# Moving the w_out sums from GpSimd to VectorE, and spacing the loads of q, k and v, in a fused attention and SiLU kernel

## The chip, the cores and the metric

The kernel runs on one core of a Trainium2 chip. The time is that of the device in microseconds (us), from several runs each; the kernel before has a median of 400.0 us in its first three runs. A profile is one execution; its span is about 1.7 us shorter than the time of the same run (381.9 against 383.64 us for the changed kernel). TensorE is PE, its weight loads PEld, VectorE DVE, ScalarE ACT, GpSimd POOL, SyncE SP.

## The reference

```python
# q, k, v: 8 batches x 12 heads x 448 positions x 64, float32
scores = (1 / sqrt(64)) * q @ k.T - log(448)
attn   = sigmoid(scores) @ v
x      = attn with heads side by side          # 3584 x 768
h      = x @ w_in                              # 768 x 2048
g      = h * sigmoid(h)
out    = g @ w_out                             # 2048 x 768, out 3584 x 768
```

## The kernel before

Groups of four heads (24 groups, numbered from 0) go through scores, sigmoid and the product with v. A batch of three groups then goes through x @ w_in, the gate, and g @ w_out. The last product is made by a scheme with seven products of quarters instead of eight. It needs sums of quarters of g, for each pair of row blocks (14 times four sums of 128x1024 on VectorE), and sums of quarters of w_out, once. The latter are eight, four for each half of the columns' chunks, and stand on GpSimd:

```python
def tt(key, dur, deps, o, a, b_, op, prio=0):
    pl.op("DVE", dur, key, deps, lambda: nc.vector.tensor_tensor(o, a, b_, op), prio=prio)

def tt_pool(key, n, deps, o, a, b_, op, prio=0):
    pl.op("POOL", 100 + 2.2 * n, key, deps, lambda: nc.gpsimd.tensor_tensor(o, a, b_, op), prio=prio)

def sums_wo(f0, f1):
    ...
    a11, a12, a21, a22 = wo[:, r, :HE], wo[:, r, HE:], wo[:, r2, :HE], wo[:, r2, HE:]
    for z, (o, x_, y_) in enumerate(((t1, a12, a11), (t2, a22, t1), (a12, a22, a12), (t4, a21, t2))):
        dz = dep if z == 0 else [kk + (z - 1,)]
        if z in (0,1,2,3):
            tt_pool(kk + (z,), (f1 - f0) * HE, dz, o, x_, y_, sub, 5)
        else:
            tt(kk + (z,), d, dz, o, x_, y_, sub, 5)
```

All loads of q, k, v and the weights are issued by GpSimd:

```python
def load(key, deps, fn, nd, size):
    first = [("issue", pl.loads)] if pl.loads else []
    pl.loads += 1
    pl.op("POOL", 650, key, deps + first, fn, nbytes=0.872 * nd / 16 * (21 + 0.0368 * size))
```

`pl` is a planner. It keeps a clock in Python, with an assumed duration for every operation, and calls each `fn` when its clock says that the operation's inputs (`deps`) are there and its engine is free. That decides only the order in which instructions enter each engine's queue. The semaphore waits of the program come from the data that instructions share (and from the reuse of semaphores), not from `deps`. This matters for the second part of the change.

## Time and profile before

| | before |
|---|---|
| time, median of the first 3 runs | 400.0 us (399.7 to 401.24) |
| PE busy, share of the span | 375.7 us, 94% |
| DVE busy | 211.1 us, 53% |
| ACT busy | 232.8 us, 58% |
| POOL busy | 90.1 us, 23% |
| mean granted clock of PE | 0.972 |

Shares of the whole span hide the point: VectorE at 53% is no bound. The prediction below therefore starts from the row of forty slices, finds the few where PE is not full, and asks what the other engines did there. One thing to know when reading busy times: an instruction that has started and is held up counts as busy all the while (the sum of 9.30 us below is one; its twins take 0.68). A "busy" VectorE can be a blocked one.

### The profile page before, as it was taken

What the parts mean: (1) busy time and instruction counts of PE and PEld (TensorE: products, weight loads), DVE (VectorE), ACT (ScalarE), POOL (GpSimd) and SP (SyncE); (2) the same over time, 40 slices, a digit from 0 to 9 for tenths busy, and PEclk for the clock granted to TensorE, in tenths of its full rate; (3) what the DMA queues carried; (4) which work ended last, traced back from release to release, by engine and by line L of the source; (5) the groups of instructions that cost most, each with busy time, mean ns of one, the idle gap of its engine ahead of it and who ended that gap; (6) DMA issues with size and microseconds to landing.
All of it is one profiled execution on the core that took longest, in us unless ns stands there. A gap on an engine that the chain in (4) does not pass through costs nothing.

```text
span 400.2 us, 17994 instructions
## 1 busy us (share of the span) xinstructions
PE 375.7 (94%) x8024; PEld 315.7 (79%) x8024; DVE 211.1 (53%) x368; ACT 232.8 (58%) x506; POOL 90.1 (23%) x105
## 2 busy tenths in 40 slices
PE   7999869995999999969999999999999999999995
PEld 3676757893887889958898889887989888988773
DVE  4536694797326447415365254554554545554633
ACT  2994629625787686445955697658647766134110
POOL 9656461892222202202022012220200000000000
PEclk9999968997999999998999999999999999999998
DMA  8999990990599996866688999988875101310235
GB/s 111 200 209 203 211 167 2 139 146 2 72 143 196 214 169 104 118 148 121 71 137 107 185 148 130 140 127 116 131 125 115 24 2 43 82 44 2 52 73 120
DMA packets 80636, 46.51 MB, mean 116 GB/s; under 512 B 50608, under 2 KB 79792, under 8 KB 80560
## 3 DMA queue, kind: packets, MB, share of 16 engines
q0 software_dynamic: 25008, 22.81, 38.4%
q1 hardware_dynamic: 55552, 22.56, 33.7%
q8 instruction: 63, 1.03, 1.0%
q14 instruction: 13, 0.11, 0.1%
HBM read 45.61 MB, written 11.01 MB: 141 GB/s over the span
## 4 chain that ended last, share of the span: by engine, by line
PE 82%; DMA 6%; DVE 5%; ACT 3%; issue 2%; POOL 0%; ACTq 0%; DVEq 0%; POOLq 0%
PE ps L803 31%; PE ps L677 29%; PE ps L502 8%; PE ps L514 8%; PE ps L713 5%; DMA xk<-in_k_dram 5%; DVE gs L276 2%; ACT at L952 2%; DVE gt L624 1%; DMA xq<-in_q_dram 1%; PE ps L985 1%; ACT sg L619 1%; PE ps L460 1%; DVE kT L474 1%; ACT at L545 0%
## 5 line engine op out<-in xcount | busy, mean ns | idle before, releaser
L677 PE MATMUL ps<-xt,wi 64*64 64x448 f16 x2304 | 166.9, 352 | 4.1 <-issue 3.7
L545 ACT ACTIVATE at<-ps 128x448 f16<-128x448 f32 x252 | 122.3, 553 | 50.8 <-PE ps L502 43.3
L677 PEld LDWEIGHTS <-wi 64*64 64x64 f16 x2304 | 114.7, 108 | 17.4 <-issue 6.1
L624 DVE TENSOR_TENSOR gt<-ps,sg 128x448 f16<-128x448 f32 (+2 forms) x128 | 78.0, 621 | 76.6 <-ACT sg L619 76.5
L803 PE MATMUL ps<-wo,gt 64*64 64x384 f16 x1344 | 114.9, 326 | 3.3 <-DVE gt L624 3.3
L803 PEld LDWEIGHTS <-gt 64*64 64x64 f16 x1792 | 98.9, 108 | 15.6 <-issue 5.9
L619 ACT ACTIVATE sg<-ps 128x448 f16<-128x448 f32 (+2 forms) x128 | 69.8, 552 | 63.9 <-PE ps L677 32.6
L803 PEld LDWEIGHTS <-gs 64*64 64x64 f16 x1344 | 78.9, 108 | 8.8 <-issue 0.7
L803 PE MATMUL ps<-so,gs 64*64 64x384 f16 x896 | 83.0, 326 | 0.0
L502 PE MATMUL ps<-qT,kT 64*64 64x448 f16 (+2 forms) x840 | 80.4, 334 | 2.2 <-DVE gt L624 1.1
L817 DVE SCALAR_TENSOR_TENSOR us<-ps,us 128x384 f32<-128x384 f32 x70 | 38.8, 555 | 56.7 <-PE ps L803 46.7
L239 POOL DMA_DIRECT2D v<-in_v_dram x24 | 17.4, 724 | 194.2 <-PE ps L514 77.8
L502 PEld LDWEIGHTS <-kT 64*64 64x64 f16 x840 | 37.5, 112 | 12.7 <-issue 8.1
L952 ACT ACTIVATE at<-ps 128x512 f16<-128x512 f32 (+3 forms) x96 | 39.6, 543 | 10.8 <-PE ps L502 10.7
L803 PE MATMUL ps<-so,gt 64*64 64x384 f16 x448 | 44.6, 323 | 0.1
L514 PE MATMUL ps<-at,v 64*64 64x448 f16 (+2 forms) x840 | 42.1, 322 | 2.7 <-DMA xk<-in_k_dram 1.5
L713 PE MATMUL ps<-xt,wi 128*128 128x256 f16 (+1 forms) x384 | 42.8, 268 | 1.4 <-issue 1.1
L803 PE MATMUL ps<-wo,gs 64*64 64x384 f16 x448 | 43.7, 323 | 0.0
L713 PEld LDWEIGHTS <-wi 128*128 128x128 f16 x384 | 34.8, 101 | 6.6 <-issue 2.8
L514 PEld LDWEIGHTS <-v 64*64 64x64 f16 x840 | 30.9, 110 | 7.3 <-issue 3.6
L824 ACT ACTIVATE us<-ps 128x384 f32<-128x384 f32 x28 | 14.0, 501 | 30.3 <-PE ps L803 30.3
L557 DVE TENSOR_SCALAR xt<-ps 128x448 f16<-128x448 f32 x36 | 20.9, 619 | 17.8 <-PE ps L514 16.2
(33 smaller groups left out, 183.8 us busy)
## 6 DMA issues: line engine op xcount, KB each, us to landing
out_dram<-us SPq DMA_DIRECT2D x112, 96.0 KB, 3.1
xk<-in_k_dram POOLq DMA_DIRECT2D x24, 224.0 KB, 6.2
v<-in_v_dram POOLq DMA_DIRECT2D x24, 224.0 KB, 5.2
xq<-in_q_dram POOLq DMA_DIRECT2D x21, 224.0 KB, 7.3
wo<-in_moe_w_out_dram POOLq DMA_DIRECT2D x4, 768.0 KB, 15.3
wi<-in_moe_w_in_dram POOLq DMA_DIRECT2D x8, 192.0 KB, 7.1
wi<-in_moe_w_in_dram POOLq DMA_DIRECT2D x4, 384.0 KB, 9.5
qT<-xq SPq DMA_TRANSPOSE x32, 4.7
```

The lines of the kernel that those rows point to most:

```text
L239: lambda: nc.gpsimd.dma_start(v16[n % NV], src(v, b, g)),
L502: nc.tensor.matmul(pt[r][64 * h : 64 * h + 64, lo : lo + (c1 - c0) * D], kT[n % NTR][64 * r : 64 * r + 64, i, 64 * h : 64 * h + 64], qT[n ...
L514: nc.tensor.matmul(pt[h][64 * j : 64 * j + 64, :N], v16[n % NV][64 * h : 64 * h + 64, j, c * D : (c + 1) * D], at[64 * h : 64 * h + 64, sl ...
L545: lambda r=r: nc.scalar.activation(at[:, sl, r], pt[r][:, :S], AF.Sigmoid, bias=NEG_LOG_S, scale=QKSCALE),
L557: lambda h=h: nc.vector.tensor_scalar_mul(x[:, 2 * g + h, :], pt[h][:, :S], SX), prio=-2,
L619: lambda: nc.scalar.activation(t[:, :ncol], src_, AF.Sigmoid, scale=ISX), prio=0,
L624: lambda: nc.vector.tensor_tensor(o, src_.rearrange("p (a t) -> p a t", a=nb), t[:, :ncol].rearrange("p (a t) -> p a t", a=nb), ALU.mult),
L677: nc.tensor.matmul(bank[64 * j : 64 * j + 64, z * N : z * N + N], wi[64 * h : 64 * h + 64, cc, f0 + 64 * j : f0 + 64 * j + 64], x[64 * h : ...
L713: nc.tensor.matmul(bank[:, z * N : z * N + N], wi[:, cc, fc * P : (fc + 1) * P], x[:, cc, self.c0 : self.c1], start=(cc == 0 and z == 0), ...
L803: nc.tensor.matmul(bank[64 * j : 64 * j + 64, :HE], lhs[64 * h : 64 * h + 64, c, 64 * j : 64 * j + 64], rhs[64 * h : 64 * h + 64, c, :], s ...
L817: lambda: nc.vector.scalar_tensor_tensor(o, bank[:, :HE], ISX, u, ALU.mult, ALU.add), prio=-2,
L952: lambda r=r, src_=src_: nc.scalar.activation(at[:, base : base + m, r, :N], src_, AF.Sigmoid, bias=NEG_LOG_S, scale=QKSCALE),
```

## The change

The intent: take the eight sums off GpSimd, and let each load from the tenth group (number 9) on be issued only when the load before has landed, so that transfers come one after another.

```diff
+    last_load = [None]
+
     def load(key, deps, fn, nd, size):
 
         first = [("issue", pl.loads)] if pl.loads else []
+        if key[0] in ("k", "q", "v") and key[1] >= 9:
+            first.append(last_load[0])
+        last_load[0] = key
         pl.loads += 1
         pl.op("POOL", 650, key, deps + first, fn, nbytes=0.872 * nd / 16 * (21 + 0.0368 * size))
@@
-            if z in (0,1,2,3):
+            if z in ():
                 tt_pool(kk + (z,), (f1 - f0) * HE, dz, o, x_, y_, sub, 5)
             else:
                 tt(kk + (z,), d, dz, o, x_, y_, sub, 5)
```

## The prediction

> **What bounds the kernel now.** I read the page's row of slices first: it says where, not only how much. Each digit is a tenth of a 10 us slice.
>
> ```profile
> PE   7999869995999999969999999999999999999995
> DVE  4536694797326447415365254554554545554633
> POOL 9656461892222202202022012220200000000000
> PEclk9999968997999999998999999999999999999998
> ```
>
> TensorE (PE) is at 9 nearly everywhere, so it is the bound. It falls to 6 in the sixth slice (50 to 60 us), to 5 in the tenth (90 to 100) and to 6 in the eighteenth, and the granted clock dips with or just after each. In the first two VectorE (DVE) and GpSimd (POOL) are both near full. The table by stretch puts numbers on it; columns are start:end, length, busy PE, PE loads, DVE, ACT, POOL with counts, clock, DMA share, GB/s.
>
> ```profile
> 45.00:57.00 12.00, 8.30 (x136) 6.79 (x136) 10.99 (x11) 5.45 (x12) 9.67 (x3) 0.85 1.17 209
> 57.00:65.00 8.00, 7.06 (x103) 5.58 (x106) 4.56 (x10) 4.87 (x11) 0.00 (x0) 0.59 0.18 29
> 65.00:82.00 17.00, 16.72 (x391) 14.16 (x380) 11.56 (x24) 12.47 (x32) 11.30 (x11) 1.00 0.70 99
> 82.00:93.00 11.00, 8.20 (x99) 8.05 (x97) 10.30 (x4) 2.07 (x4) 10.47 (x4) 1.00 0.89 107
> 93.00:101.00 8.00, 6.36 (x59) 3.82 (x61) 4.95 (x11) 5.51 (x12) 0.00 (x0) 0.58 0.01 2
> ...
> 184.00:370.00 186.00, 185.22 (x4108) 163.12 (x4102) 95.52 (x164) 115.30 (x246) 17.95 (x25) 1.00 0.63 97
> ```
>
> From 184 to 370 us PE is busy 99.6%: nothing to gain there. Twice before 101 us a stretch with idle PE is followed by one at 0.59 or 0.58 of the clock. In 82 to 93 us DVE completes only 4 instructions in 10.3 us. The timeline of DVE, then of POOL, says why.
>
> ```profile
> 49.87 3.44 DVE L276 TENSOR_TENSOR gs<-gs,gt 128x1024 f16<-128x1024 f16 x1
> ...
> 53.71 3.11 DVE L276 TENSOR_TENSOR gt<-gt 128x1024 f16<-128x1024 f16 x1
> 56.74 0.68 DVE L276 TENSOR_TENSOR gs<-gt,gs 128x1024 f16<-128x1024 f16 x1
> ...
> 83.72 9.30 DVE L276 TENSOR_TENSOR gs<-gt 128x1024 f16<-128x1024 f16 x1
> ```
>
> ```profile
> 49.68 3.09 POOL L279 TENSOR_TENSOR so<-wo,so 128x1536 f16<-128x1536 f16 x1 [0.75 <-DMA wo<-in_moe_w_out_dram]
> ...
> 80.24 6.16 POOL L279 TENSOR_TENSOR so<-wo,so 128x1536 f16<-128x1536 f16 x2
> 86.35 3.09 POOL L279 TENSOR_TENSOR wo<-wo 128x1536 f16<-128x1536 f16 x1
> 89.39 3.07 POOL L279 TENSOR_TENSOR so<-wo,so 128x1536 f16<-128x1536 f16 x1
> ```
>
> The same DVE sum of 128x1024 takes 0.68 us alone and 3 to 9 us beside POOL's w_out sums. The one of 9.30 us ends at 93.02, just after POOL's last sum (89.39 + 3.07 = 92.46) plus its own 0.6. So POOL's sums cost PE time through DVE, which also empties PSUM. The list of waits agrees:
>
> ```profile
> PE ps L803 <- DVE gt L624: 3.3, 1, 3.3
> PE ps L460 <- DVE gt L624: 2.3, 1, 2.3
> PE ps L514 <- DMA xk<-in_k_dram: 1.5, 1, 1.5
> ```
>
> I read the third as DVE too. The built program has that matmul wait for DVE, and it starts at 57.94, 0.06 us after the gate product (L624, 57.34 + 0.54) that frees its bank; what its weights need was loaded from 29.77 us on.
>
> [...] It works the other way too: POOL's third sum took 3.54 instead of 3.09 us. [...]
>
> **The change part by part.** *Second part first.* The kernel's streams are ordered by a planner with its own clock; "issued when its predecessor has landed" is added only to what the planner waits for. In the built changed kernel GpSimd's loads come in the same sequence, and their semaphore waits are of the same kinds as before: the eighth load back, the engine that reads the buffer, its transposes. No load waits for its predecessor. What moves is order: on PE, DVE and ACT only between about 59 and 158 us, and on SyncE output stores of the first blocks go ahead of some transposes of groups 10 and 11. Those transposes still stand seven or more score steps ahead of the matmuls that need them, each step some 2 us of PE. Worth: 0, give or take 1 us.
>
> *First part, removed.* 8 sums on POOL (12.3 + 6.6 + 6.2 = 25.1 us). POOL was not the bound, so by itself this is nothing. What counts is the blocking of DVE: 1.57 + 3.44 + 3.11 - 3 x 0.68 = 6.1 us in the first stretch, 9.30 - 0.68 = 8.6 us in the second.
>
> *Stretch A, 45 to 65 us.* PE's transposes at 53.84 waited 2.33 us for a gate product queued behind a blocked sum. Unblocked, DVE starts sums 0.60 us apart and gate products 0.46 apart: from 47.92 us it comes to that product at about 49.6, ends it at 50.1, and PE need not wait at 51.5. The next bank is free at about 51.8, so the matmuls of 57.94 start at about 53.0: 5.0 us earlier. The work from 57.94 to 63.29 (5.35 us) ran at half clock. Warm, its parts take 0.96 + 0.63 + 1.05 + 0.5 = 3.1 and small gaps, say 3.3: 2 us more. Sum A: 7.0 us.
>
> *Stretch B, 82 to 101 us.* PE stops at 90.2 with every bank waiting for DVE and resumes at 93.55: 3.35 us. From there to 101 (7.45 us) the clock is 0.58, with 1.1 us of further waits for the gate backlog. At full clock that is about (7.45 - 1.1) x 0.58 = 3.7 us: 3.7 us saved. Sum B: 7.0 us.
>
> *Added.* 8 sums of 128x1536 on DVE: [...] 0.95 us each, 7.6 us busy; they start some 0.87 apart (0.60 + 0.27), 7.0 us of the queue. All stand after the last clean gs sum and before the next set, about 55 to 68 us on the new clock. By then w_out has landed: its transfers, issued from 34.83, were followed in the queue by a k load that landed at about 58, and the second half is wanted only at about 61. Between 57 and 82 us DVE has 4.56 + 11.56 = 16.1 us of busy time; with 7.6 that is 23.7 in a stretch that shrinks to some 23. Busy times overlap by about 0.08 us an instruction, so it just fits, but DVE is nearly full. Working down its queue at these spacings I find the gate products up to 2.6 us behind PE's pace near 64 us, and level again by 75. Eight banks hide most of it; I charge 1 us, with 3 possible. The sums are done some 15 us before their first product.
>
> Sum: 400.0 - 7.0 - 7.0 + 1.0 = 387.0 us.
>
> **The rivals.** *DVE becomes the bound between 55 and 75 us.* For it: 23.7 us of work in 23. Against: the overlap, and idle DVE until 80 to catch up in. If PE then waits 3 us and its clock falls again (another 3 to 4), A is given back: about 393. *The stalls move to data.* DMA runs at 200 GB/s and over until 57 us; PE arriving 5 to 7 us early could wait for k and q of the seventh group, which land near 58 to 60, or the v loads behind them. Against: those are first used after about 62, and loads then go out on an idle queue (29 GB/s in 57 to 65). If it bites, 2 to 3 us: about 390. *The 3.06 us stop at 175.6 us moves.* No engine or transfer that the profile shows ends it, and the clock dips after it (0.88 in 170 to 184). The instruction order there is the same as before, so I keep it. Gone, it would give some 4 us: 383; doubled by the new timing, 391. *GpSimd free earlier speeds up the loads.* It held one v load back by about 1 us behind a sum at 71 us; the others waited for PE. Nothing.
>
> **Range and chances.** The two stalls are read directly and removed at the root, so I am sure of the sign; the size depends on whether the clock stays up. 383 to 392 covers one such accident either way. 2% is 392.0. Faster by over 2%: 0.88; within: 0.11; slower: 0.01.
>
> **What would show it.** Right: no DVE sum over about 1.1 us anywhere; PE at 9 in the slices that now hold 6 and 5, with the clock near 1; the eight new sums at about 0.95 us; the list of waits without the 3.3 and 2.3. DVE at 9 around 55 to 70 us, with PE at 9 beside it. Wrong: PE waits for DVE there of over 2 us in all, or a second stretch at half clock (the first rival); [...] a stop after 100 us that the old trace lacks (then the reordering costs, and the second part is not worth 0).

## The result

The changed kernel takes 386.1 us (median of 4 runs, 383.64 to 388.13) against 400.62 us for the kernel before in all its runs up to then (4 runs, 399.7 to 403.27). The ratio is 0.9625, 95% interval 0.9551 to 0.9698: faster by 3.75%. Ratios here are the mean time of one kernel's fast runs over that of the other's in the same rounds, so they are not quite the ratios of the medians quoted.

The profiled run is the fastest of the four. Three rows of its slices (lines of the changed kernel carry numbers higher by 5):

```profile
PE   6999899999999999999999999999999999999995
DVE  3545699863355465263643546454654446464623
PEclk9999999999999999999999999999999999999998
```

The 6 and the 5 that marked the two stalls are gone, the clock stays at 9 up to the last slice, and VectorE has its 9s in the sixth and seventh slices (48 to 67 us; a slice is 9.5 us now), where the eight sums went. By stretch:

```profile
45.00:57.00 12.00, 11.13 (x221) 9.07 (x224) 10.86 (x22) 8.69 (x20) 0.00 (x0) 1.00 1.16 210
57.00:65.00 8.00, 7.40 (x167) 5.54 (x165) 7.54 (x14) 6.98 (x20) 2.06 (x3) 1.00 0.34 52
...
75.00:87.00 12.00, 12.00 (x167) 10.78 (x168) 7.60 (x14) 7.24 (x16) 0.00 (x0) 1.00 0.87 104
```

Compare the first line with the same stretch before: VectorE's busy time is nearly the same (10.86 against 10.99 us), but it does 22 instructions in place of 11. PE runs 221 matmuls in place of 136. The timeline of VectorE shows what became of the long sums:

```profile
49.02 0.68 DVE L281 TENSOR_TENSOR gs<-gs,gt 128x1024 f16<-128x1024 f16 x1
...
55.08 0.95 DVE L281 TENSOR_TENSOR so<-wo 128x1536 f16<-128x1536 f16 x1
...
77.32 0.69 DVE L281 TENSOR_TENSOR gs<-gt 128x1024 f16<-128x1024 f16 x1
```

The sums of 3.44 and 9.30 us take 0.68 and 0.69; a moved one takes 0.95. The two longest waits of PE that remain have nothing to do with VectorE's sums:

```profile
PE ps L465 <- DMA xk<-in_k_dram: 1.8, 2, 1.1
PE ps L990 <- DVE warm L199: 1.2, 1, 1.2
```

Where the time came from can be read by following the same PE instruction through both traces (starts in us, from the timeline and the chain of work that ended last):

| PE instruction | before | after | gained so far |
|---|---|---|---|
| product with v after the first stall | 57.94 | 52.92 | 5.0 |
| gate-input matmuls at the end of the slow clock | 63.29 | 55.80 | 7.5 |
| start of the row of 132 matmuls | 78.18 | 71.77 | 6.4 |
| first product with w_out | 93.55 | 83.73 | 9.8 |
| product with v of group 6 | 105.47 | 91.28 | 14.2 |
| product with v of group 11 | 165.27 | 150.48 | 14.8 |
| product with v of group 12 | 185.10 | 166.44 | 18.7 |
| product with v of group 23 | 339.48 | 321.34 | 18.1 |

All of the gain but one step is made by 105 us. The step between groups 11 and 12 is the 3.06 us stop of the old trace at 175.6 us and the slow clock behind it (granted 0.50 from 179.7 to 183.1 us). Stops for which the profile shows no cause turn up in other traces at other places: 2.00 us at 116.6 in the run with the first part alone, 2.94 at 124.2 in the run that keeps the old order. So I count it as chance. It is in the difference of the two profiled spans (18.3 us). Without its 3.9 us (18.7 - 14.8) they differ by 14.4 us, as the medians do (14.5 us).

Busy totals confirm the reading: VectorE falls from 211.1 to 203.6 us although eight sums were added. Taking off the blocked time of the prediction (6.1 + 8.6) and adding eight sums (7.6) gives 204.

### The profile page after: what moved, and what is told of

Its sections match the earlier page's. It is cut to its first block, busy times and chain, and to the rows that moved or that the text cites. A ratio compares the mean times of both kernels' runs of the same rounds, so it can differ in the third digit from the quotient of the medians.

```text
span 381.9 us, 17992 instructions
## 1 busy us (share of the span) xinstructions
PE 368.6 (97%) x8024; PEld 306.9 (80%) x8024; DVE 203.6 (53%) x376; ACT 232.2 (61%) x506; POOL 65.1 (17%) x97
## 4 chain that ended last, share of the span: by engine, by line
PE 90%; ACT 4%; issue 2%; DMA 1%; POOL 1%; DVE 0%; ACTq 0%; POOLq 0%; DVEq 0%
PE ps L808 33%; PE ps L682 29%; PE ps L718 10%; PE ps L507 9%; PE ps L519 8%; ACT at L957 3%; DMA xk<-in_k_dram 1%; PE ps L465 1%; ACT at L550 1%; ACT sg L624 1%; PE ps L990 1%; POOL xk L224 0%; POOL xq L233 0%; DVE us L822 0%; DVE xt L979 0%
## 5 line engine op out<-in xcount | busy, mean ns | idle before, releaser
L808 PE MATMUL ps<-wo,gt 64*64 64x384 f16 x1344 | 111.8, 323 | 0.6 <-issue 0.6
L808 PEld LDWEIGHTS <-gt 64*64 64x64 f16 x1792 | 95.5, 107 | 13.2 <-issue 2.1
L624 ACT ACTIVATE sg<-ps 128x448 f16<-128x448 f32 (+2 forms) x128 | 70.3, 554 | 51.4 <-PE ps L682 30.6
L808 PEld LDWEIGHTS <-gs 64*64 64x64 f16 x1344 | 76.1, 107 | 10.1 <-issue 1.0
L808 PE MATMUL ps<-so,gs 64*64 64x384 f16 x896 | 81.3, 323 | 0.0
L507 PE MATMUL ps<-qT,kT 64*64 64x448 f16 (+2 forms) x840 | 79.5, 325 | 1.4 <-ACT at L957 0.4
L957 ACT ACTIVATE at<-ps 128x512 f16<-128x512 f32 (+3 forms) x96 | 39.7, 562 | 10.2 <-PE ps L507 10.2
L808 PE MATMUL ps<-so,gt 64*64 64x384 f16 x448 | 45.6, 323 | 0.0
L718 PE MATMUL ps<-xt,wi 128*128 128x256 f16 (+1 forms) x384 | 40.8, 260 | 1.1 <-issue 1.1
L718 PEld LDWEIGHTS <-wi 128*128 128x128 f16 x384 | 33.1, 98 | 5.8 <-issue 2.5
```

What stands on the lines that cost most here:

```text
L507: nc.tensor.matmul(pt[r][64 * h : 64 * h + 64, lo : lo + (c1 - c0) * D], kT[n % NTR][64 * r : 64 * r + 64, i, 64 * h : 64 * h + 64], qT[n ...
L624: lambda: nc.scalar.activation(t[:, :ncol], src_, AF.Sigmoid, scale=ISX), prio=0,
L718: nc.tensor.matmul(bank[:, z * N : z * N + N], wi[:, cc, fc * P : (fc + 1) * P], x[:, cc, self.c0 : self.c1], start=(cc == 0 and z == 0), ...
L808: nc.tensor.matmul(bank[64 * j : 64 * j + 64, :HE], lhs[64 * h : 64 * h + 64, c, 64 * j : 64 * j + 64], rhs[64 * h : 64 * h + 64, c, :], s ...
L957: lambda r=r, src_=src_: nc.scalar.activation(at[:, base : base + m, r, :N], src_, AF.Sigmoid, bias=NEG_LOG_S, scale=QKSCALE),
```

## The experiments

Ten kernels ran, all with a correct result, three rounds each, beside runs of the kernel before. The line numbers in their traces shift with each edit; the names of the tiles tell which instruction it is. The medians are over all runs, those marked slow too; the ratios use fast runs alone.

| run | median us | ratio to before, 95% interval |
|---|---|---|
| part1_alone | 389.72 | 0.9641 (0.9555 to 0.9727) |
| part2_alone | 402.5 | 1.0028 (1.0000 to 1.0056) |
| before_order_dve | 387.98 | 0.9677 (0.9620 to 0.9735) |
| after_idle_reads | 401.53 | 0.9985 (0.9948 to 1.0021) |
| after_idle_writes | 388.22 | 0.9689 (0.9617 to 0.9761) |
| first_half_dve | 392.66 | 0.9825 (0.9749 to 0.9901) |
| before_pieces | 395.71 | 0.9901 (0.9869 to 0.9933) |
| after_true_wait | 399.79 | 0.9925 (0.9875 to 0.9975) |
| before_self_wait | 399.54 | 0.9923 (0.9886 to 0.9961) |
| idle_reads_free | 403.0 | 1.0021 (0.9990 to 1.0052) |

At the 2% of the record, part1_alone, before_order_dve and after_idle_writes are faster, first_half_dve is unclear (its interval reaches from 1 to 2.5%), and the other six are the same. Of these six, before_pieces, after_true_wait and before_self_wait are still below 1 by the whole interval.

### Each part alone

```diff
 part1_alone (from the kernel before)
-            if z in (0,1,2,3):
+            if z in ():
 part2_alone (from the changed kernel)
-            if z in ():
+            if z in (0,1,2,3):
```

> Only the w_out sums go to VectorE; the planner's wait for the previous load is left out. Built, its TensorE order is that of the changed kernel but for a handful of waits, since that wait exists in the planner only. My theory (all the gain is the lifted block between GpSimd and VectorE): 386 us, within 2 of the changed kernel. Rival (the spacing of the loads earns part of it): 390 us or more.

> Only the planner's wait; the sums stay on GpSimd. My theory: 400 us, within 2 of the kernel before, with a VectorE sum of about 9 us still in the trace. Rival (loads spaced out help): 396 us or less.

Measured: 389.72 us (384.91 to 391.98, 4 runs), ratio 0.9641, and 402.5 us, ratio 1.0028. The first median is above my 388, but two of its four runs are marked slow (the fast ones are 384.91 and 388.29), its ratio lies inside the changed kernel's interval, and its trace has an unexplained stop of 2.00 us that the changed kernel's lacks. The first part carries the gain. The second is worth nothing that these runs can tell; if anything 0.3% slower. The long sum is still there with the second part alone (this profile fell in a slow run, so only the instruction is compared, not the span):

```profile
83.47 9.39 DVE L281 TENSOR_TENSOR gs<-gt 128x1024 f16<-128x1024 f16 x1
```

The built programs say the same (my count; the files of the runs do not hold the built programs). With waits included, PE's queue of some 16,000 rows shows 6 lines of difference between the first part alone and the changed kernel, and 6 between the second part alone and the kernel before.

### The engine without the new order

```diff
 before_order_dve (from the kernel before, in tt_pool)
-        ... lambda: nc.gpsimd.tensor_tensor(o, a, b_, op), prio=prio)
+        ... lambda: nc.vector.tensor_tensor(o, a, b_, op), prio=prio)
```

> The order of the kernel before on every engine, with each of the eight sums issued to VectorE at the place where the planner had put it on GpSimd; nothing else moves. My theory: the engine alone makes the gain, 386 to 389 us; a little worse than the changed kernel is possible, as the sums stand where GpSimd would have had them. Rival (the new order of TensorE's work makes the gain): 395 us or more.

Measured: 387.98 us, ratio 0.9677. The planner still believes that the sums are on GpSimd, so the order of all other work is the old one, and the gain is there all the same. What the planner rearranged in the changed kernel is not the cause.

### GpSimd kept busy: reading, then writing

This is the test of the mechanism. Every other engine keeps the changed kernel's instructions and waits; only GpSimd gets useless work back, where the sums had been in its queue.

```diff
 after_idle_reads (from the changed kernel, shortened; called after q loads of groups 6, 7, 9: 3, 1, 4 times)
+    nc.gpsimd.tensor_tensor(pd, wo[:, f0 : f0 + 4, :HE], wo[:, HFC + f0 : HFC + f0 + 4, :HE], ALU.subtract)
 after_idle_writes
+    nc.gpsimd.tensor_tensor(pd[:, :8], ...)      # waits for the same w_out load
+    nc.gpsimd.memset(pd, 0.0)                    # 3400 elements
```

> The changed kernel, plus eight useless subtractions on GpSimd of the old size (128x1536, two inputs from w_out, output to a scratch tile that nobody reads), at the places in GpSimd's queue where the old sums stood. All other engines keep the changed kernel's instructions and waits. My theory (GpSimd's reads block VectorE's two-input sums): both stalls come back, and since VectorE now has more two-input sums there, 398 to 408 us with VectorE sums of 3 us and more. Rival (what cost time was that the sums' results came late, or that loads queued behind them): 386 to 388 us.

> As the run with eight useless subtractions on GpSimd, but each is replaced by a fill of 3400 f16 elements of the scratch tile (an estimate of 3 us each from the 204 ns of the 128-wide fill of the identity tile), behind an 8-element subtraction that makes it wait for the same w_out load. GpSimd is busy as long and in the same places, but hardly reads SBUF. My theory[...]: no block, VectorE sums of 0.7 and 0.95 us, 386 to 389 us. Rival (any long GpSimd instruction holds VectorE up, or delays the loads behind it enough to matter): 395 us or more.

No trace before this run showed VectorE beside a long fill; the theory was an assumption of mine.

Measured: 401.53 us with reads, 388.22 us with writes. With reads the whole gain is gone, although nobody needs their results and VectorE does the real sums. The timelines of VectorE (first stretch, then second) and of GpSimd in that run, and PE's longest wait, which is that of the first stretch:

```profile
51.28 3.11 DVE L291 TENSOR_TENSOR gt<-gt 128x1024 f16<-128x1024 f16 x1
...
85.69 3.24 DVE L291 TENSOR_TENSOR gs<-gt 128x1024 f16<-128x1024 f16 x1
...
89.32 3.11 DVE L291 TENSOR_TENSOR gs<-gs,gt 128x1024 f16<-128x1024 f16 x1
```

```profile
82.11 13.26 POOL L226 TENSOR_TENSOR pd<-wo 128x1536 f16<-128x1536 f16 x4
```

```profile
PE ps L529 <- DVE gt L639: 5.2, 1, 5.2
```

And the same two with writes: a VectorE sum that starts, and ends, in the middle of a fill (78.10 to 81.03 us):

```profile
79.10 0.68 DVE L290 TENSOR_TENSOR gs<-gs,gt 128x1024 f16<-128x1024 f16 x1
```

```profile
78.10 2.93 POOL L227 MEMSET pd<- 128x3400 f16 x1
```

The eight fills keep GpSimd busy for 23.4 us (8 x 2.93), as long as the sums did (25.1), and hold its queue up as much. VectorE's sums stay at 0.68 to 0.96 us throughout. So it is neither a busy GpSimd nor loads queued behind it. In these two runs what held up a VectorE sum with two inputs in SBUF was a GpSimd instruction that reads SBUF: sums of 128x1024 take up to 3.56 us beside the subtractions, 0.68 us beside the fills. An instruction of VectorE with one input in SBUF was not drawn out in the kernel before: the gate product (L624, one input in PSUM, one in SBUF) at 83.00 took 0.69 us, the same as the mean of its kind in the changed kernel (686 ns), although GpSimd's sums ran from 80.24 to 92.46 us.

### One half of the sums

```diff
 first_half_dve (from the kernel before, in tt_pool)
-        ... nc.gpsimd.tensor_tensor(o, a, b_, op)
+        ... (nc.vector if key[1] == 0 else nc.gpsimd).tensor_tensor(o, a, b_, op)
```

> The order of the kernel before, with the four sums of the first half of w_out issued to VectorE and the four of the second half left on GpSimd. My theory of two separate stalls of some 7 us each: the one at 50 to 65 us goes, the one at 83 to 101 us stays, 393 to 395 us. Rival (the first stall's time is only pushed into the second, or either half alone is enough): 399 or 388 us.

Measured: 392.66 us, ratio 0.9825, 0.3 us under the range that I gave. That is 1.75% of 400.41, or 7.0 us, for the first half; with both halves in the same order it was 3.23% of 401.31, or 13.0 us, so 6.0 us for the second. So the first stall can go without the second. That the two add up is not shown: the 6.0 us are a remainder, no run moved the second half alone, and the interval for the first half reaches from 4 to 10 us. The victim in the second stretch is now another sum, one of the moved ones, blocked by three of those left on GpSimd:

```profile
74.25 9.85 DVE L279 TENSOR_TENSOR so<-wo,so 128x1536 f16<-128x1536 f16 x1
```

### Shorter GpSimd sums

```diff
 before_pieces (from the kernel before, in tt_pool)
-        ... nc.gpsimd.tensor_tensor(o, a, b_, op)
+        ... [nc.gpsimd.tensor_tensor(o[:, c], a[:, c], b_[:, c], op) for c in range(4)]
```

> The kernel before with each GpSimd sum of 128x1536 cut into four of 128x384, 32 in all; the order is unchanged elsewhere. [...] a VectorE sum waits 0.8 us at most, not 3 to 9: VectorE sums of 1.5 us at most and 388 to 394 us. If it holds VectorE off through a row of its instructions, as the 9.30 us sum across three of them suggests: sums of several us again, 398 us or more.

The first of the two cases is that VectorE gets in between two pieces; its 0.8 us is an estimate, a quarter of the 3.09 us that a whole GpSimd sum takes in the trace before.

Measured: 395.71 us, ratio 0.9901, between my two cases. In the first stretch VectorE's four sums take 0.72 to 1.40 us: it gets in between pieces. In the second it does not:

```profile
77.86 10.14 DVE L276 TENSOR_TENSOR gs<-gt 128x1024 f16<-128x1024 f16 x1
```

GpSimd ran sums without a break from 74.38 to 88.75 us, and VectorE's sum ended at 88.00. Cutting work into pieces let VectorE in during one stretch and not during the other.

### Does a row of GpSimd sums hold VectorE off?

The VectorE sum of 9.30 us in the kernel before lasted until three GpSimd sums in a row had ended. Beside the four useless subtractions of the second stretch, three VectorE sums took 3.24, 3.11 and 3.10 us: VectorE got in after one subtraction each time. The theory of the row, a guess to be tested: VectorE gets in between two GpSimd sums only when the second has to wait on a semaphore for the first. To find out when VectorE gets in, one run makes every old GpSimd sum wait for the one before it, and one gives the useless subtractions four scratch tiles in turn, so that none waits for its predecessor.

```diff
 before_self_wait (from the kernel before, after each GpSimd sum s)
+        tc.add_manual_dep(s, last_sum, ...)      # a semaphore wait between two GpSimd sums
 idle_reads_free (from after_idle_reads)
-    pd = sb("pd", [PD], F16)
+    pd = [sb(f"pd{i}", [PD], F16) for i in range(4)]
```

> The kernel before, with each GpSimd sum made to wait on a semaphore for the GpSimd sum before it (in the kernel before only some of them wait, and for sums long done). Other engines unchanged. [...] Theory of the back-to-back row: [...] Then no VectorE sum is over 4 us here, the second stall shrinks, and the time falls to 392 to 397 us. Rival (it has to do with something else in that stretch): a sum of 9 us again and 400 us.

> As the run with eight useless subtractions, but with four scratch tiles in turn, so that none waits for the one just before it. Theory of the back-to-back row: [...] one sum of 9 us or more at 83 to 95 us, and a time of 402 us or more, over the 401.5 of that run. Rival: VectorE gets in after each, sums of 3 us, 398 to 402 us as in that run.

Measured: 399.54 and 403.0 us. In the second stretch the instructions went as the theory of the row has it. The sum of 9.30 us becomes 3.35 with the wait, and the 3.24 us one of the run with useless reads becomes 9.20 without it. First the run with the wait, then the run without:

```profile
83.84 3.35 DVE L276 TENSOR_TENSOR gs<-gt 128x1024 f16<-128x1024 f16 x1
```

```profile
85.34 9.20 DVE L291 TENSOR_TENSOR gs<-gt 128x1024 f16<-128x1024 f16 x1
```

My expected time for the first was wrong: 399.54, not 392 to 397. VectorE gets in after one GpSimd sum, and its next two sums, at 87.57 and 91.07 us, are then blocked for 3.11 and 3.10 us in turn. That is 9.6 us for the three, against 9.30 + 0.68 + 0.68 = 10.7 in the kernel before. The waiting was mostly dealt out differently. For the second, 403.0 us lies in the range given and above the other run's 401.53, but the ranges of single runs and the intervals of the ratios overlap. What decides when VectorE gets in stays open. In the first stretch two GpSimd sums of the kernel before follow each other without such a wait (49.68 and 52.72 us), and VectorE did get in between them (its 3.44 us sum); the same happens in part2_alone (3.14 us) and idle_reads_free (3.12 us). And in the second stretch of part2_alone GpSimd issued a load of 0.74 us before each of its last two sums (at 84.65 and 88.45 us), and VectorE's sum waited through both sums all the same (9.39 us).

### The wait of the second part, made real

```diff
 after_true_wait (from the changed kernel, in load, for k, q, v of group 9 and later)
+        tc.add_manual_dep(this_load, load_before, ...)   # a semaphore wait in GpSimd's queue
```

> The changed kernel with the wait that its words speak of made real: each load of q, k and v from the tenth group on waits on a semaphore until the load before it has landed. All other engines keep their instructions and waits. My theory (the planner's wait is not in the program): this run is different from the changed kernel, loads of one group leave some 5 to 7 us apart instead of 0.7. As a group of heads takes some 14 us of TensorE and three loads of 5 to 7 us one after another take 15 to 20, the loads become the bound of the second half: 400 to 440 us. Rival (loads are issued far enough ahead, so it is hidden): 386 to 390 us.

Measured: 399.79 us, ratio 0.9925, at the low end of what I expected. It gives nearly all of the gain back. GpSimd's queue, with what ended its idle time in brackets:

```profile
106.50 0.72 POOL L258 DMA_DIRECT2D v<-in_v_dram  x1 [4.91 <-PE ps L822]
113.22 0.71 POOL L238 DMA_DIRECT2D xk<-in_k_dram  x1 [6.01 <-DMA v<-in_v_dram]
117.26 0.71 POOL L247 DMA_DIRECT2D xq<-in_q_dram  x1 [3.32 <-DMA xk<-in_k_dram]
```

Loads of a group leave 4 to 7 us apart; in the changed kernel they leave 0.7 us apart (101.23, 101.94, 102.65). PE pays in its longest wait, for transposed q:

```profile
PE ps L521 <- DMA qT<-xq: 13.4, 6, 4.8
```

So the second part, taken by its words, would cost some 12 us (ratios 0.9925 and 0.9625, a difference of 0.030 of 400 us); the wait itself does not exist in the program. No variant beat the changed kernel.

## Why the prediction was right

387.0 us was predicted, 386.1 measured, and the steps can be checked one by one. That the total is so near is in part luck: the gain was 1.5 us larger than predicted (14.5 against 13.0 between the medians), and 0.6 us of this went into a median before of 400.62 us in place of 400.0.

- **The cause.** VectorE sums blocked by GpSimd's reads: shown. Useless reads bring the stalls back (VectorE sums of up to 3.56 us), useless writes of about the same length do not (0.68 to 0.96 us).
- **Stretch A.** Predicted 5.0 us at the first product after the stall and 7.0 with the clock; the traces give 5.0 and 7.5. So the wait was sized right and the slow clock 0.5 us too small.
- **The charge for the added sums.** Predicted 1.0 us lost to a nearly full VectorE between 55 and 75 us. The gain shrinks from 7.5 to 6.4 us between 55.80 and 71.77, so 1.1 us. The sums ran from 55.08 to 68.91 us at 0.95 us each, where the prediction had 55 to 68 and 0.95. (That 0.95 was my estimate; the trace before has no sum of 128x1536 on VectorE that would show it.) But the trace does not put this loss on VectorE. From 46 us to the end it shows no wait of PE for VectorE. In the 16 us in question PE waits once for a named engine, 0.25 us for ScalarE at 57.62. ScalarE is busy without a break from 54.14 to 62.5 us, and the chain of work that ended last runs over its sigmoids (L957 and L624) from 54.15 to 60.05. So the size was right by luck, and the reason given for it is not what the trace shows. The first rival did not come true: the granted clock is 1.00 in 45 to 87 us.
- **Stretch B.** Predicted 7.0 us, 3.35 for the wait and 3.7 for the clock. The gain grows from 6.4 to 14.2 us, 7.8 in all: 3.4 by the first product with w_out and 4.4 after it. The clock's term was sized 0.7 us too small.
- **The second part.** Predicted 0, within 1 us; the run with it alone is at ratio 1.0028 (up to 0.6% slower by the interval), and making it real costs some 12 us, so the reading that it never enters the program was the right one. One detail was wrong: under this part I listed the new order of PE's work between 59 and 158 us. That order comes from the first part; of PE's rows the second moves only a handful. The order of SyncE's stores and transposes, which I listed too, does move with the second part alone.
- **The other rivals.** The stalls did not move to data: after 46 us PE's waits name no transfer. (Its two waits for k, 1.8 us, end at 5.10 and 8.61 us, at the start of the program.) The stop at 175.6 us was gone from the profiled run, worth some 4 us there, and stops of 1 to 4 us appear at other places in other runs, so I take it as part of the spread and not of the change.
- **A reading that was wrong.** Under the row of slices I wrote that VectorE and GpSimd are both near full in the sixth and the tenth. The row has 9 and 6, and 7 and 2. It is in the stretches of 45 to 57 and 82 to 93 us that both are near full.

The sum, 7.0 + 7.0 - 1.0 = 13.0 us, compares with 14.2 us in the traces at group 6 and with 14.5 us between the medians.

## What to carry to other kernels

When an instruction's duration in the trace is several times that of its twins, look for what ran on the other engines at the same time before looking at data or queues (here GpSimd's sums: 9.30 us against 0.68); the fix may be to give the work to the engine that was "busy" only because it was blocked. Move work off a helper engine even when that engine is idle most of the time, if its instructions hold up the engine that frees the bound engine's buffers (GpSimd was busy for 23% of the span here, and the changed kernel is 14.5 us faster). And when a scheduler orders the program, check in the built program whether a wait is a wait or only an order: here the one that was meant would have undone the gain.

## What these traces show of GpSimd beside VectorE, and of the clock

- A VectorE sum of 128x1024, which takes 0.68 us alone, waited through two further GpSimd sums (9.30 us; in part2_alone 9.39 us, with a load issued before each of them), and through a row of short ones (10.14 us). It got in after one when each GpSimd sum waited on a semaphore for the one before (3.35 us, and 3.24 us beside useless reads). The row does not explain every case, since in the first stretch of three runs VectorE got in between two GpSimd sums without such a wait (3.44, 3.14 and 3.12 us). Inside a fill of 2.93 us it took 0.68 us.
- In the trace before, the granted clock is 0.50 in three stretches of 10.2, 6.8 and 3.4 us (53.4 to 63.6, 94.3 to 101.2, 179.7 to 183.1). 12 matmuls of 128x192 take 1.16 us before the first of them and 2.10 in it. In the 3.4 us before the three, PE was busy for 1.5, 0.5 and 1.0 us; in the last 3.4 us of each it was busy throughout. The two waits of the first stall, 2.3 and 1.5 us, came with 10.2 us at half clock. How much idle time brings the clock down, and what sets the length of such a stretch, these traces do not show.
- Blocked time counts as busy in the profile's share of VectorE; here it was 14.7 us of 211.1.
